# Two-expert routing: dense products over all tokens replaced by rows scattered to, and gathered from, per-expert parts of DRAM

## The chip, the core and the metric

One core of a Trainium2 chip runs the program. The metric is the device time of one execution in microseconds (us); the kernel before takes 2873.46 us, the median of 3 runs (2871.51 to 2873.73).

## The reference

A delta-rule attention (4 batches, 8 heads, 768 steps, head width 48) gives 3072 tokens of 384 numbers. A router chooses two of eight experts for each token, and each chosen expert adds its weighted two-layer product. All is float32.

```python
# attention, per step t
y[:, :, t] = einsum('bhd,bhde->bhe', q[:, :, t], state)
state = state + bt * einsum('bhd,bhe->bhde', kt, vt - v_old)
# router, N = 3072, D = 384, E = 8, F = 1024
noisy = x @ w_gate + log1p(exp(x @ w_noise)) * noise
top2 = argpartition(-noisy, 2, axis=1)[:, :2]        # softmax over the two: top2_w
for e in range(E):
    for k in range(2):
        mask = top2[:, k] == e
        h = maximum(x[mask] @ w1[e], 0.0)
        out[mask] += top2_w[mask, k, None] * (h @ w2[e])
```

The inputs are seeded. Counted from the reference on them, the eight experts are chosen by 711, 771, 789, 774, 756, 744, 807 and 792 tokens.

## The kernel before

Stage 1 is `deltanet` (lines 152 to 426): 24 groups (6 chunks of 128 tokens by 4 batches, the chunk the outer loop), three in flight at a time, advanced in turns by generators. For a group, `load` (186) brings k, q and v by SP's DMA queue into one of five buffer sets, `prepare` (202) normalizes the keys on POOL and VectorE (DVE), and `group` (240) builds an inverse of a 128 by 128 triangular matrix per head by merging blocks: TensorE (PE) products `p_m` (line 297) alternate with DVE operations that mask or add them (315, 305, 327). POOL adds the identity once a group (284). The group's result `y` is copied by ScalarE (ACT, 388), transposed on PE (`p_xt`, 394) and stored in `xT`, which holds all 3072 tokens, transposed, on chip.

Stage 2 is the router (lines 431 to 499): 72 products `p_l` (437), each of which PE runs as two instructions, then one chain of some 30 DVE and ACT operations on 128 by 24 by 8 numbers, which ends in `gate`, the weight of each expert for each token, 0 for all but two.

Stage 3 is the experts (lines 501 to 541): for each of 8 experts and each of 6 blocks of 512 tokens, the first product `p_h` (515; 24 products of 512 columns, 48 instructions) with a relu on ACT (521), then the second product `p_o` (526; 32 products of 384 columns, 64 instructions), which DVE adds to `acc` with the gate (532, 536). Weights of the next expert are loaded while one is computed (`load_weights`, 128). With the last expert each 128 tokens of `acc` are stored (541).

Each engine and each DMA-issuing queue runs its instructions in the order in which the scheduler of the framework wrote them; an instruction that waits holds those behind it. PSUM tiles (`ps`) rotate through 8 banks.

Of the kernel before, what the change touches and what calls it, by code (L numbers as in the profile page):

```python
# [20 lines left out]
TT = 512  # tokens in a tile of the experts' first product  # L21
# [3 lines left out]
def kernel(  # L25
# [49 lines left out]
    # 1 where the row is before the column  # L75
# [7 lines left out]
    # the two diagonal blocks of a pair of heads' state  # L83
# [5 lines left out]
    # -1 for rows in the lower block of a pair, by the columns of its upper block; 0 for  # L89
    # those of its lower block  # L90
# [16 lines left out]
    # -1 for even rows, by the next column  # L107
# [9 lines left out]
    # expert index less E, for the choice of the first of equal logits  # L117
# [4 lines left out]
    xT = const.tile([128, KT, N], FP32, name="xT")  # L122

# [28 lines left out]
    def deltanet(ictx):  # L152
# [31 lines left out]
        state = {}  # L184

# [22 lines left out]
            # normalized keys; a Newton step takes the square root to full precision  # L208
# [31 lines left out]
        def group(n):  # L240
# [4 lines left out]
            # two heads to a transpose  # L245
# [11 lines left out]
            # A^T, by parity of the heads: they stand in different rows of the array  # L257
# [13 lines left out]
            # the inverse of I + A, block by block, and its transpose  # L271
# [39 lines left out]
            for s in LEVELS:  # L311
                x = sb([128, H, 128], "x", IN_FLIGHT)  # - E T
# [19 lines left out]
            # strictly lower part of Q K^T, transposed  # L332
# [54 lines left out]
            y = sb([128, H, D], "y", 2)  # L387
# [7 lines left out]
            tok0 = b * S + c * C  # L395
            nc.scalar.copy(xT[:, :, tok0 : tok0 + C], p_xt)

        for n in range(n_sets):
            load(n)
        load_router()  # L400
        prepare(0)
# [30 lines left out]
    work = ctx.enter_context(tc.tile_pool(name="route", bufs=1))  # L432
    wgn, noise = router["wgn"], router["noise"]
    p_l = ps([128, NT, 2, E], "p_l")
    for t in range(NT):
        for do in range(KT):
            nc.tensor.matmul(  # L437
                p_l[:, t], xT[:, do, t * 128 : (t + 1) * 128], wgn[:, do],
                start=(do == 0), stop=(do == KT - 1),
            )  # L440

    def full(name):
        return work.tile([128, NT, E], FP32, name=name)

    def per_token(name):
        return work.tile([128, NT], FP32, name=name)

    def over_experts(t):
        return t[:, :, None].to_broadcast([128, NT, E])

    def vv(out, a, b, op):
        nc.vector.tensor_tensor(out=out, in0=a, in1=b, op=op)

    # log(1 + exp(z)) = max(z, 0) + log1p(exp(-|z|)); log1p corrected for 1 + u's rounding
    z_pos, u, w, d, noisy = (full(x) for x in ("z_pos", "u", "w", "d", "noisy"))
    nc.scalar.activation(u, p_l[:, :, 1], ACTF.Abs)
    nc.scalar.activation(u, u, ACTF.Exp, scale=-1.0)
    nc.vector.tensor_scalar_max(z_pos, p_l[:, :, 1], 0.0)
    nc.vector.tensor_scalar_add(w, u, 1.0)
    nc.vector.tensor_scalar_sub(d, w, 1.0)  # L460
    vv(d, u, d, ALU.subtract)
    nc.vector.reciprocal(noisy, w)
    vv(d, d, noisy, ALU.mult)
    nc.scalar.activation(w, w, ACTF.Ln)
    vv(w, w, d, ALU.add)
    vv(w, w, z_pos, ALU.add)
    vv(w, w, noise, ALU.mult)
    vv(noisy, w, p_l[:, :, 0], ALU.add)

    def take_largest(x, name):  # L470
        """The largest logit of each token, and 1 for the first expert that has it."""
        top, at, hit = per_token(f"{name}_top"), per_token(f"{name}_at"), full(f"{name}_hit")
        nc.vector.tensor_reduce(out=top, in_=x, axis=AX.X, op=ALU.max)
        vv(hit, x, over_experts(top), ALU.is_equal)
        code_b = code[:, None, :].to_broadcast([128, NT, E])
        vv(hit, hit, code_b, ALU.mult)
        nc.vector.tensor_reduce(out=at, in_=hit, axis=AX.X, op=ALU.min)
        vv(hit, code_b, over_experts(at), ALU.is_equal)
        return top, hit

    top0, hit0 = take_largest(noisy, "a")
    rest = full("rest")
    nc.vector.scalar_tensor_tensor(
        out=rest, in0=hit0, scalar=-1e30, in1=noisy, op0=ALU.mult, op1=ALU.add
    )
    top1, hit1 = take_largest(rest, "b")
    p1, den = per_token("p1"), per_token("den")
    vv(p1, top1, top0, ALU.subtract)
    nc.scalar.activation(p1, p1, ACTF.Exp)
# [4 lines left out]
    vv(p1, p1, den, ALU.mult)
    gate = full("gate")
    vv(gate, hit0, over_experts(den), ALU.mult)
    vv(hit1, hit1, over_experts(p1), ALU.mult)
    vv(gate, gate, hit1, ALU.add)

# [1 line left out]
    w_odd = ctx.enter_context(tc.tile_pool(name="w_odd", bufs=1))  # L501
    hid = ctx.enter_context(tc.tile_pool(name="hid", bufs=2))
    acc_pool = ctx.enter_context(tc.tile_pool(name="acc", bufs=1))
    acc = acc_pool.tile([128, NT, DM], FP32, name="acc")

    for e in range(E):
# [3 lines left out]
        for tt in range(N // TT):  # L510
            hT = hid.tile([128, FT, TT], FP32, name="hT")
            for fo in range(FT):
                p_h = ps([128, TT], "p_h")
                for do in range(KT):
                    nc.tensor.matmul(  # L515
                        p_h,
                        w1e[:, do, fo * 128 : (fo + 1) * 128],
                        xT[:, do, tt * TT : (tt + 1) * TT],
                        start=(do == 0), stop=(do == KT - 1),
                    )  # L520
                nc.scalar.activation(hT[:, fo], p_h, ACTF.Relu)  # L521
            for i in range(TT // 128):
                t = tt * (TT // 128) + i
                p_o = ps([128, DM], "p_o")
                for fo in range(FT):
                    nc.tensor.matmul(  # L526
                        p_o, hT[:, fo, i * 128 : (i + 1) * 128], w2e[:, fo],
                        start=(fo == 0), stop=(fo == FT - 1),
                    )
                g = gate[:, t, e : e + 1]  # L530
                if e == 0:
                    nc.vector.tensor_scalar(  # L532
                        out=acc[:, t], in0=p_o, scalar1=g, scalar2=None, op0=ALU.mult
                    )
# [38 lines left out]
```

## Time and profile before

| | us |
|---|---|
| median of 3 runs (2871.51 to 2873.73) | 2873.46 |
| span of the profiled execution, first to last instruction | 2872.1 |
| stage 1, delta rule, until the first product of the router | 855.9 |
| stage 2, router products on PE | 30.5 |
| stage 3, experts, until the last product | 1982.1 |
| PE busy | 2826.4 (98%) |
| DVE, ACT, POOL busy | 712.0, 340.0, 157.0 |

The profile is one execution on the chip. The span of the profiled execution is its own time but for 1.4 us, the difference to the median. A busy share is an average over stages with different limits, so a stage is read by the stretch of time that it takes. In the chain that ended last, a row is a piece of work of one engine which the next piece waited for.

### The profile page before, as it was taken

What the parts mean: (1) busy time and instruction counts of PE and PEld (TensorE: products, weight loads), DVE (VectorE), ACT (ScalarE), POOL (GpSimd) and SP (SyncE); (2) the same over time, 40 slices, a digit from 0 to 9 for tenths busy, and PEclk for the clock granted to TensorE, in tenths of its full rate; (3) what the DMA queues carried; (4) which work ended last, traced back from release to release, by engine and by line L of the source; (5) the groups of instructions that cost most, each with busy time, mean ns of one, the idle gap of its engine ahead of it and who ended that gap; (6) DMA issues with size and microseconds to landing.
All of it is one profiled execution on the core that took longest, in us unless ns stands there. A gap on an engine that the chain in (4) does not pass through costs nothing.

```text
span 2872.1 us, 28617 instructions
## 1 busy us (share of the span) xinstructions
PE 2826.4 (98%) x12894; PEld 1849.6 (64%) x12894; DVE 712.0 (25%) x1279; ACT 340.0 (12%) x610; POOL 157.0 (5%) x183
## 2 busy tenths in 40 slices
PE   5999999999999999999999999999999999999999
PEld 5999999999996555555555555555555555555555
DVE  5766677777651000000000000000000000000000
ACT  1111111111101110011001101110111011101110
POOL 3111221111000000000000000000000000000000
PEclk9999999999997999999999999999999999999999
DMA  5010100000000001000100100000010000000000
GB/s 94 18 23 18 21 18 18 18 18 12 1 22 23 0 1 44 0 0 0 44 0 0 44 0 0 22 22 1 0 44 0 0 22 22 0 0 6 17 22 22
DMA packets 93915, 46.10 MB, mean 16 GB/s; under 512 B 79424, under 2 KB 90688, under 8 KB 93792
## 3 DMA queue, kind: packets, MB, share of 16 engines
q1 hardware_dynamic: 93792, 44.27, 5.9%
q8 instruction: 101, 1.65, 0.2%
q14 instruction: 22, 0.18, 0.0%
HBM read 39.54 MB, written 4.72 MB: 15 GB/s over the span
## 4 chain that ended last, share of the span: by engine, by line
PE 93%; DVE 3%; POOL 2%; issue 1%; ACT 0%; POOLq 0%; DVEq 0%; ACTq 0%
PE p_h L515 35%; PE p_o L526 34%; PE p_m L297 17%; POOL w_inv L284 2%; PE p_g L265 2%; PE p_u L354 1%; PE p_l L437 1%; DVE w_inv L278 1%; PE p_t L250 1%; DVE t_inv L290 1%; PE p_b L347 1%; ACT at L277 0%; PE p_xt L394 0%; PE p_y L382 0%; DVE w_inv L327 0%
## 5 line engine op out<-in xcount | busy, mean ns | idle before, releaser
L515 PE MATMUL p_h<-xT,w1e 128*128 128x512 f32 x2304 | 999.1, 593 | 0.0
L526 PE MATMUL p_o<-w2e,hT 128*128 128x384 f32 x3072 | 998.6, 486 | 0.0
L526 PEld LDWEIGHTS p_o<-w2e,hT 128*128 128x128 f32 x3072 | 583.8, 190 | 417.1 <-issue 23.0
L515 PEld LDWEIGHTS p_h<-xT,w1e 128*128 128x128 f32 x2304 | 438.7, 190 | 541.9 <-issue 529.5
L536 DVE SCALAR_TENSOR_TENSOR acc<-p_o,gate,acc 128x384 f32<-128x384 f32 x168 | 103.8, 618 | 1628.3 <-PE p_o L526 1628.3
L521 ACT ACTIVATE hT<-p_h 128x512 f32<-128x512 f32 x384 | 229.3, 597 | 1727.3 <-PE p_h L515 1727.3
L297 PE MATMUL p_m<-t_inv,at 128*128 128x128 f32 x2304 | 283.4, 279 | 25.3 <-DVE t_inv L290 25.3
L297 PEld LDWEIGHTS p_m<-t_inv,at 128*128 128x128 f32 x2304 | 269.9, 194 | 29.2 <-issue 29.2
L297 PE MATMUL p_m<-x,w_inv 128*128 128x128 f32 x1920 | 233.3, 277 | 1.4 <-DVE x L315 1.4
L297 PEld LDWEIGHTS p_m<-x,w_inv 128*128 128x128 f32 x1920 | 222.4, 192 | 2.6 <-DVE x L315 2.0
L315 DVE TENSOR_TENSOR x<-p_m,neg 128x512 f32<-128x512 f32 x288 | 195.9, 686 | 107.6 <-PE p_m L297 107.4
L327 DVE STREAM_TRANSPOSE w_inv<-t_inv 128x1024 f32<-128x1024 f32 x96 | 119.2, 1242 | 2.1
L305 DVE TENSOR_TENSOR t_inv<-p_m,t_inv 128x256 f32<-128x256 f32 x240 | 96.4, 414 | 52.2 <-PE p_m L297 50.4
L297 PE MATMUL p_m<-w_inv,x 128*128 128x128 f32 x768 | 93.7, 275 | 0.0
L297 PEld LDWEIGHTS p_m<-w_inv,x 128*128 128x128 f32 x768 | 89.6, 192 | 0.1
L532 DVE TENSOR_SCALAR acc<-p_o,gate 128x384 f32<-128x384 f32 x24 | 14.8, 618 | 221.4 <-PE p_o L526 221.4
L252 ACT COPY kT<-p_t 128x512 f32<-128x512 f32 x24 | 14.2, 591 | 468.3 <-PE p_t L250 468.3
L284 POOL TENSOR_TENSOR w_inv<-w_inv,ident 128x1024 f32<-128x1024 f32 x24 | 56.4, 2352 | 155.5 <-DVE w_inv L278 153.7
L382 PE MATMUL p_y<-u,qk 128*128 128x48 f32 x384 | 47.5, 278 | 0.0
L382 PEld LDWEIGHTS p_y<-u,qk 128*128 128x128 f32 x384 | 46.5, 198 | 0.0
L305 DVE TENSOR_TENSOR w_inv<-p_m,w_inv 128x256 f32<-128x256 f32 x96 | 37.7, 411 | 18.7 <-PE p_m L297 18.7
L354 PE MATMUL p_u<-r,w_inv 128*128 128x48 f32 x320 | 37.8, 271 | 0.8 <-DVE r L349 0.8
(109 smaller groups left out, 820.2 us busy)
## 6 DMA issues: line engine op xcount, KB each, us to landing
w1e<-in_moe_w_dram SPq DMA_DIRECT2D x8, 1536.0 KB, 6.4
w2e<-in_moe_w_dram SPq DMA_DIRECT2D x8, 1536.0 KB, 7.1
kp<-in_k_dram SPq DMA_DIRECT2D x24, 192.0 KB, 2.8
qp<-in_q_dram SPq DMA_DIRECT2D x24, 192.0 KB, 2.8
vr<-in_v_dram SPq DMA_DIRECT2D x24, 192.0 KB, 2.7
out_dram<-acc SPq DMA_DIRECT2D x24, 192.0 KB, 1.9
beta_sb<-in_beta_dram SPq DMA_DIRECT2D x1, 96.0 KB, 2.2
noise<-in_moe_noise_dram SPq DMA_DIRECT2D x1, 96.0 KB, 3.8
```

The costliest lines, as they stand in the source:

```text
L265: nc.tensor.matmul(p_g[par][:, j], kT[lo : lo + DP, j], rhs[lo : lo + DP, j])
L284: nc.gpsimd.tensor_tensor(out=w_inv, in0=w_inv, in1=ident[:, None, :].to_broadcast([128, H, 128]), op=ALU.add,)
L297: nc.tensor.matmul(p[:, i], lhsT[:, h0 + i], rhs[:, h0 + i])
L305: nc.vector.tensor_tensor(out=to, in0=halves(p, s)[low], in1=to, op=ALU.add)
L315: lambda p, hs: nc.vector.tensor_tensor(out=x[:, hs], in0=p, in1=neg[s][:, None, :].to_broadcast([128, NP, 128]), op=ALU.mult,),
L327: nc.vector.transpose(out=w_flat, in_=t_flat)
L354: nc.tensor.matmul(p_u[:, h], w_inv[:, h], r[:, h])
L382: nc.tensor.matmul(p_y[:, h], qk[:, h], u[:, h], start=(st is None and h == 0), stop=(h == H - 1), skip_group_check=True,)
L515: nc.tensor.matmul(p_h, w1e[:, do, fo * 128 : (fo + 1) * 128], xT[:, do, tt * TT : (tt + 1) * TT], start=(do == 0), stop=(do == KT - 1),)
L521: nc.scalar.activation(hT[:, fo], p_h, ACTF.Relu)
L526: nc.tensor.matmul(p_o, hT[:, fo, i * 128 : (i + 1) * 128], w2e[:, fo], start=(fo == 0), stop=(fo == FT - 1),)
L536: nc.vector.scalar_tensor_tensor(out=acc[:, t], in0=p_o, scalar=g, in1=acc[:, t], op0=ALU.mult, op1=ALU.add,)
```

## The change

`TILES` is 7, `HALF` 448 and `TT` 512. The router moves into stage 1, where it runs once per chunk (512 tokens), and the experts multiply only the rows sent to them.

- `rows_x` and `rows_y` are DRAM buffers of 8 parts with 3072 rows of 384 numbers. `clear` (new) writes zeros to the first 896 rows of each part of `rows_x` and to the other 2176 rows of each part of `rows_y`: 64 stores, 24576 rows of 1536 bytes, issued by SP after the router's loads and ahead of the first weights.
- `group` ends with its own 3 router products `p_l`. With the last batch of a chunk, `route` (new) runs the router's chain on 128 by 4 by 8 numbers, finds each token's row among its expert's rows (`before` counts the earlier ones; two products `p_at` with a triangular and an all-ones matrix count those of the same chunk), and `spread` (new) sends `y` by 8 indirect DMAs of 128 rows each, issued by POOL. `xT` is 3 buffers of one group instead of all tokens; `y` has 8 buffers.
- An expert loads its 896 rows (`xr`), which waits for all 48 scatters, transposes them by 21 PE transposes, and runs the first product on two halves of 448 columns (48 products) and the second on 7 tiles (56 products of 384 columns). DVE copies each result, and SP stores it to `rows_y`.
- A branch for experts with over 896 rows: every engine loads the largest count and, if it is above 896, the other 17 tiles of each of the 8 experts are computed.
- At the end POOL gathers, for each of 24 tiles of tokens, two tiles of 128 rows by indirect DMAs; ACT and DVE weight and add them, and SP stores them.

```diff
+    def clear(e):
+        for i in range(TILES):
+            r0 = e * N + i * 128
+            cleared.append(nc.sync.dma_start(out=rows_x[r0 : r0 + 128], in_=zero).ins)
+        left = rows_y[e * N + TILES * 128 : (e + 1) * N]
+        nc.sync.dma_start(out=left.rearrange("(t p) d -> p t d", p=128),
+            in_=zero[:, None, :].to_broadcast([128, NT - TILES, DM]))
+    def spread(rows, slot):
+        d = nc.gpsimd.indirect_dma_start(out=rows_x,
+            out_offset=bass.IndirectOffsetOnAxis(ap=slot, axis=0),
+            in_=rows, in_offset=None).ins
...
+        for i in cleared:
+            tc.add_manual_dep(d, i.name, SYNC, reason="rows cleared before they are written")
+        def route(c):
...
+            vv(taken, hit0, hit1, ALU.add)
+            for i in range(B):
+                nc.vector.tensor_copy(earlier[:, i], before)
+                vv(before, before, taken[:, i], ALU.add)
+            nc.tensor.matmul(p_at, mask_u, taken, start=True, stop=False)
+            nc.tensor.matmul(p_at, ones, earlier, start=False, stop=True)
+            vv(at, p_at, part[:, None, :].to_broadcast([128, B, E]), ALU.add)
+            for hit, slot in ((hit0, slots[0]), (hit1, slots[1])):
+                vv(mine, hit, at, ALU.mult)
+                nc.vector.tensor_reduce(out=row, in_=mine, axis=AX.X, op=ALU.add)
+                nc.vector.tensor_copy(slot[:, to], row)
+            for b in range(B):
+                for slot in slots:
+                    spread(ys[n], slot[:, n : n + 1])
...
-            nc.scalar.copy(xT[:, :, tok0 : tok0 + C], p_xt)
+            nc.scalar.copy(xT, p_xt)
+            for do in range(KT):
+                nc.tensor.matmul(p_l, xT[:, do], wgn[:, do], ...)
+            nc.scalar.copy(logits[c][:, b], p_l)
+            if b == B - 1:
+                route(c)
...
         load_router()
+        for e in range(E):
+            clear(e)
         prepare(0)
         first_weights = load_weights(w_even, 0)
...
     for e in range(E):
-        for tt in range(N // TT):
...
+        d = nc.sync.dma_start(out=xr, in_=rows_x[rows].rearrange("(t p) d -> p t d", p=128)).ins
+        for i in written:
+            tc.add_manual_dep(d, i.name, SYNC, reason="rows of all tokens")
+        for i in range(TILES):
+            transposed(xr, xe, i)
+        for h0 in range(0, TILES * 128, HALF):
+            first(w1e, xe, hT, slice(h0, h0 + HALF))
+        for i in range(TILES):
+            second(w2e, hT, i, yr)
+            nc.sync.dma_start(out=rows_y[r0 : r0 + 128], in_=yr)
+    count = nc.values_load(most_i[0:1, 0:1], min_val=0, max_val=N)
+    with tc.If(count > TILES * 128):
...
+    for c in range(NCH):
+        for b in range(B):
+            for slot in slots:
+                nc.gpsimd.indirect_dma_start(out=g, in_=rows_y, ...)
+            nc.scalar.mul(got[0], got[0], gates[0][:, n : n + 1])
+            nc.vector.scalar_tensor_tensor(out=got[0], in0=got[1], scalar=gates[1][:, n : n + 1], ...)
+            nc.sync.dma_start(out=out[t0 : t0 + C, :], in_=got[0])
```

How the order moves, at three places. First, SP's queue at the start, before (`w1e` and `w2e` are the weights of expert 0; `qp`, `vr` and `kp` behind them belong to group 5 and later):

```order
L146 DMA noise<-in_moe_noise_dram 128x24x8
L131 DMA w1e<-in_moe_w_dram 128x3x1024
L132 DMA w2e<-in_moe_w_dram 128x8x384
L191 DMA qp_124<-in_q_dram 128x8x48
L191 DMA qp_128<-in_q_dram 128x8x48
L191 DMA qp_132<-in_q_dram 128x8x48
L191 DMA vr<-in_v_dram 128x8x48
L191 DMA kp_123<-in_k_dram 128x8x48
```

The same place in the change, from the last of the eight pairs of clearing rows on:

```order
L186 DMA rows_x<-zero 128x384 x7
L188 DMA rows_y<-zero 128x17x384
L159 DMA w1e<-in_moe_w_dram 128x3x1024
L160 DMA w2e<-in_moe_w_dram 128x8x384
L334 DMA kp_145<-in_k_dram 128x8x48
L334 DMA qp_146<-in_q_dram 128x8x48
L334 DMA vr<-in_v_dram 128x8x48
```

All 64 clearing stores stand ahead of the weights and of the loads of group 5; each DMA of SP also waits for the landing of the one that stands eight before it.

Second, PE where the last group of the first chunk ends, before (`p_m` belongs to the next two groups):

```order
L394 MATMUL p_xt<-ident,y 128x128 x3
L297 MATMUL p_m<-t_inv,at 128x128 x8
L297 MATMUL p_m<-x,w_inv 128x128 x16
L297 MATMUL p_m<-w_inv,x 128x128 x8
L297 MATMUL p_m<-t_inv,at 128x128 x16
```

and in the change:

```order
L537 MATMUL p_xt<-ident,y 128x128 x3
L440 MATMUL p_m<-t_inv,at 128x128 x8
L440 MATMUL p_m<-x,w_inv 128x128 x8
L545 MATMUL p_l<-wgn,xT 128x16 x3
L306 MATMUL p_at<-r_taken,mask_u 128x32
L440 MATMUL p_m<-x,w_inv 128x128 x2
L307 MATMUL p_at<-r_earlier,ones 128x32
L440 MATMUL p_m<-x,w_inv 128x128 x6
L440 MATMUL p_m<-w_inv,x 128x128 x8
L440 MATMUL p_m<-t_inv,at 128x128 x16
```

The product `p_at` stands right behind `p_l`, so PE waits there for `r_taken`, which 24 DVE operations of the chain compute behind `p_l`; on DVE the chain's 41 operations stand together, with one transpose of another group among them, and the `t_inv` additions that the last row's products need come behind them. The same happens in five chunks; in the sixth nothing else is left to do.

Third, SP where the experts begin, in the change:

```order
L334 DMA kp_157<-in_k_dram 128x8x48
L159 DMA w1e<-in_moe_w_dram 128x3x1024
L160 DMA w2e<-in_moe_w_dram 128x8x384
L625 DMA xr<-rows_x 128x7x384 x3
L159 DMA w1e<-in_moe_w_dram 128x3x1024
L640 DMA rows_y<-yr 128x384 x6
```

The weights of expert 1 take memory that stage 1 held, and their load waits for all its readers, the scatters too; the rows of experts 0, 1 and 2 stand behind these weights, two experts ahead of their use from then on.

## Rows read from the trace of the kernel before

**Rows 1.** The page: span, and busy time of each engine.

```profile
span 2872.1 us, 28617 instructions
...
PE 2826.4 (98%) x12894; PEld 1849.6 (64%) x12894; DVE 712.0 (25%) x1279; ACT 340.0 (12%) x610; POOL 157.0 (5%) x183
```

**Rows 2.** Chain that ended last, by time: start us, us, work.

```profile
855.90 30.53 PE p_l L437 x144
886.43 23.09 PE p_h L515 x48
909.52 20.64 PE p_o L526 x64
930.16 20.60 PE p_h L515 x48
...
2847.80 20.66 PE p_o L526 x64
```

**Rows 3.** Windows: busy us (count) of PE, PEld, DVE, ACT, POOL; clock; DMA; GB/s.

```profile
200.00:300.00 100.00, 99.28 (x913) 97.34 (x912) 71.02 (x129) 12.85 (x27) 18.80 (x17) 1.00 0.10 19
...
850.00:870.00 20.00, 19.37 (x94) 19.21 (x93) 0.00 (x0) 1.22 (x3) 0.00 (x0) 0.50 0.45 157
```

**Rows 4.** Groups by line and form: busy us, mean ns, idle before.

```profile
L297 PE MATMUL p_m<-t_inv,at 128*128 128x128 f32 x2304 | 283.4, 279 | 25.3 <-DVE t_inv L290 25.3
...
L437 PE MATMUL p_l<-wgn,xT 128*128 128x16 f32 x144 | 30.7, 373 | 0.0
...
L394 PE MATMUL p_xt<-ident,y 128*128 128x128 f32 x72 | 12.2, 280 | 0.6 <-ACT y L388 0.6
...
L388 ACT COPY y<-p_y 128x384 f32<-128x384 f32 x24 | 11.5, 479 | 61.8 <-PE p_y L382 61.8
```

**Rows 5.** Timeline of the router's chain on DVE and ACT: start us, us, instruction.

```profile
886.60 0.33 ACT L456 ACTIVATE u<-p_l 128x192 f32<-128x192 f32 x1 [30.18 <-PE p_l L437]
886.95 1.28 ACT L457 ACT_TABLE_LOAD   x1
...
892.15 1.28 ACT L464 ACT_TABLE_LOAD   x1
...
900.39 0.36 DVE L452 TENSOR_TENSOR gate<-gate,b_hit 128x192 f32<-128x192 f32 x1
```

**Rows 6.** Timeline of DVE in stage 1: two dependent small operations.

```profile
94.30 0.16 DVE L220 TENSOR_TENSOR rec<-rec,ss 128x8 f32<-128x8 f32 x1
94.50 0.17 DVE L221 TENSOR_TENSOR rec<-rec,root 128x8 f32<-128x8 f32 x1
```

**Rows 7.** Timeline of POOL in stage 1.

```profile
88.39 0.82 POOL L210 TENSOR_TENSOR ksq<-kp 128x384 f32<-128x384 f32 x1 [0.30 <-DMA kp<-in_k_dram]
...
178.71 0.83 POOL L231 TENSOR_TENSOR kb<-kp,beta_t 128x384 f32<-128x384 f32 x1 [15.72 <-PE p_t L250]
...
219.85 2.35 POOL L284 TENSOR_TENSOR w_inv<-w_inv,ident 128x1024 f32<-128x1024 f32 x1 [5.36 <-DVE w_inv L278]
...
232.21 0.83 POOL L227 TENSOR_TENSOR kp<-kp,ksc 128x384 f32<-128x384 f32 x1 [8.26 <-DVE ksc L226]
247.04 0.83 POOL L231 TENSOR_TENSOR kb<-kp,beta_t 128x384 f32<-128x384 f32 x1 [14.01 <-PE p_t L250]
```

**Rows 8.** SP's DMA issues at the start: start us, us, what is loaded.

```profile
19.38 2.00 SPq L131 DMA_DIRECT2D w1e<-in_moe_w_dram  x1
...
84.86 0.37 SPq L191 DMA_DIRECT2D kp<-in_k_dram  x1
```

**Rows 9.** DMA of the window 855 to 875 us: rate in 40 slices, issues, us to landing.

```profile
GB/s 0 0 0 0 131 66 238 401 418 410 418 442 410 373 402 396 375 381 369 369 384 298 12 0 0 0 0 0 0 0 0 0 0 0 0 33 0 0 0 0
...
w2e<-in_moe_w_dram SPq DMA_DIRECT2D x1, 1536.0 KB, 10.2
```

**Rows 10.** Line 541, the output's stores: issue ns min/median/max, and time to landing.

```profile
L541 SPq DMA_DIRECT2D out_dram<-acc x24: 332/332/366, 2647.4 to 2869.1; - x24
...
DMA to landing us min/median/max: 1.8/1.9/2.0
```

**Rows 11.** The page's DMA issues: KB each, median us from issue to landing.

```profile
kp<-in_k_dram SPq DMA_DIRECT2D x24, 192.0 KB, 2.8
```

More of the change, by code (lines that the diff above doesn't have):

```diff
@@ L149, in load_router @@
         router["wgn"], router["noise"] = wgn, noise
+    cleared, written = [], []
+    def clear(e):
[3 more added lines that the diff above has]
+        left = rows_y[e * N + TILES * 128 : (e + 1) * N]
+        nc.sync.dma_start(
+            out=left.rearrange("(t p) d -> p t d", p=128),
+            in_=zero[:, None, :].to_broadcast([128, NT - TILES, DM]),
+        )
+    def spread(rows, slot):
+        d = nc.gpsimd.indirect_dma_start(
+            out=rows_x,
+            out_offset=bass.IndirectOffsetOnAxis(ap=slot, axis=0),
+            in_=rows,
+            in_offset=None,
+        ).ins
+        tc.declare_no_dep(d, group="spread", reason="no two tokens have the same row")
+        tc.add_to_no_dep_group("spread", d)
+        for i in cleared:
+            tc.add_manual_dep(d, i.name, SYNC, reason="rows cleared before they are written")
+        written.append(d)
     def deltanet(ictx):
@@ L400, in deltanet @@
         load_router()
+        for e in range(E):
+            clear(e)
         prepare(0)
@@ L429, with transposed @@
         weights = deltanet(ictx)
[L432 to L435, printed above, removed]
+    w_odd = ctx.enter_context(tc.tile_pool(name="w_odd", bufs=1))
+    moe = ctx.enter_context(tc.tile_pool(name="moe", bufs=2))
+    def transposed(xr, xe, i):
+        p_xt = ps([128, KT, 128], "p_xt")
         for do in range(KT):
+            nc.tensor.transpose(p_xt[:, do], xr[:, i, do * 128 : (do + 1) * 128], ident)
+        nc.vector.tensor_copy(xe[:, :, i * 128 : (i + 1) * 128], p_xt)
@@ new lines, in first, with second @@
+    def first(w1e, xe, hT, cols):
+        for fo in range(FT):
+            p_h = ps([128, cols.stop - cols.start], "p_h")
+            for do in range(KT):
+                nc.tensor.matmul(
+                    p_h, w1e[:, do, fo * 128 : (fo + 1) * 128], xe[:, do, cols],
+                    start=(do == 0), stop=(do == KT - 1),
+                )
+            nc.scalar.activation(hT[:, fo, cols], p_h, ACTF.Relu)
+    def second(w2e, hT, i, yr):
+        p_o = ps([128, DM], "p_o")
+        for fo in range(FT):
@@ L455 @@
[L455 to L465, printed above, removed]
@@ L494 @@
[L494 to L504, printed above, removed]
+                p_o, hT[:, fo, i * 128 : (i + 1) * 128], w2e[:, fo],
@@ L506 @@
+                start=(fo == 0), stop=(fo == FT - 1),
+            )
+        nc.vector.tensor_copy(yr, p_o)
     for e in range(E):
@@ L509 @@
             weights = load_weights(w_odd if e % 2 == 0 else w_even, e + 1)
-        for tt in range(N // TT):
[L511 to L534, printed above, removed]
-                else:
-                    nc.vector.scalar_tensor_tensor(
-                        out=acc[:, t], in0=p_o, scalar=g, in1=acc[:, t],
-                        op0=ALU.mult, op1=ALU.add,
-                    )
-                if e == E - 1:
-                    nc.sync.dma_start(out=out[t * 128 : (t + 1) * 128, :], in_=acc[:, t])
@@ new lines @@
+    nc.vector.tensor_reduce(out=most, in_=p_n, axis=AX.X, op=ALU.max)
+    nc.vector.tensor_copy(most_i, most)
+    count = nc.values_load(most_i[0:1, 0:1], min_val=0, max_val=N)
+    with tc.If(count > TILES * 128):
+        more = NT - TILES
+        w1f = moe_w1.rearrange("e d f -> (e d) f")
+        w2f = moe_w2.rearrange("e f d -> (e f) d")
+        for e in range(E):
+            with tc.tile_pool(name=f"left{e}", bufs=1) as pool:
+                w1e = pool.tile([128, KT, F], FP32, name="w1l")
+                w2e = pool.tile([128, FT, DM], FP32, name="w2l")
+                nc.sync.dma_start(out=w1e, in_=w1r[e])
+                nc.sync.dma_start(out=w2e, in_=w2r[e])
+                for i in range(TILES, NT):
+                    r0 = e * N + i * 128
+                    xr = pool.tile([128, 1, DM], FP32, name="xrl")
+                    nc.sync.dma_start(out=xr[:, 0], in_=rows_x[r0 : r0 + 128])
+                    xe = pool.tile([128, KT, 128], FP32, name="xel")
+                    transposed(xr, xe, 0)
+                    hT = pool.tile([128, FT, 128], FP32, name="hTl")
+                    first(w1e, xe, hT, slice(0, 128))
+                    yr = pool.tile([128, DM], FP32, name="yrl")
+                    second(w2e, hT, 0, yr)
+                    nc.sync.dma_start(out=rows_y[r0 : r0 + 128], in_=yr)
```

151 lines of the change are left out of this document (112 added, 39 removed).

## Prediction

> **What bounds the kernel now.** I read the page first: PE is busy for 98% of the span [rows 1]. A share over the whole span says little, so the chain by time comes next [rows 2]. From 855.90 us on there is one piece of PE work behind another: the router's products until 886.43, then blocks of 20.60 us (`p_h`) and 20.64 us (`p_o`) that alternate, 48 of each, until 2868.46. That is 1982 us of experts, or 69% of the span, with nothing but PE in the chain. Last come the windows by stage [rows 3]: in stage 1 PE is busy for 99.28 of 100 us while DVE has 71.02 and POOL 18.80, so PE sets the pace there too, but only because the other engines come back in time. Small transfers, POOL and ACT cost nothing now. The change takes most of the PE work away and puts waits between engines in its place, so the question is how much of 1982 us the waits give back.
>
> **What goes.** Everything after 855.90 us [rows 2], 2016.2 us of the profiled span.
>
> **The experts that come.** Work is now 896 rows an expert and not 3072. A block's 24 products of 512 columns take 20.60 us; 48 products of 448 columns take 2 x 20.60 x 448/512 = 36.05 us. 32 products of 384 columns take 20.64 us; 56 take 36.12 us. 21 transposes at 12.2 us / 72 = 0.17 us [rows 4] are 3.6 us. With 0.6 us until the first copies of the transposed rows are there, an expert is 76.4 us and eight are 611 us. Loads and copies beside it are covered: rows and weights come two experts ahead, and 5.9 MB in 76 us is 78 GB/s where 369 to 442 GB/s are to be had [rows 9]. If that cover went, an expert would wait up to 10.2 us, a weight load's landing. After a stretch at clock 0.50 [rows 3], the lower of the two levels (1.2 GHz), the first block took 23.09 us in place of 20.60 [rows 2]; PE idles before the experts again, so I add 2.5 us. **614 us.**
>
> **The router's products inside stage 1.** 144 instructions in 30.7 us at clock 0.50 [rows 3, 4] are 0.21 us each, so some 0.107 at full clock, 15.3 us in all on PE, which has no room. With 12 small `p_at`: **16 us.** Bounds: 8 us if gaps take half of it, 31 at the low clock.
>
> **The chain that PE waits for in five chunks.** PE stands at `p_at` right behind `p_l`. Before it come ACT's copy and Abs (0.3 us each) and a table load of 1.28 us [rows 5], Exp (0.3), 24 DVE operations and a wait of some 0.7 us for the second table. Dependent DVE operations of 8 columns follow each other at 0.20 us (94.30 to 94.50 [rows 6]); for 32 columns I take 0.22, so 5.3 us. That is 8.2 us. The other 16 operations (3.5 us) still hold DVE while PE has 16 products, 3.9 us at 2 x 0.123 (283.4/2304 [rows 4]), so they hide. Behind DVE's chain are the other groups' additions; I add 2 us for catching up: 10 us, **50 us** for five. Bounds: 5 us a chunk if other work fills half; 14.2 us, the whole chain of before (886.60 to 900.75 [rows 5]).
>
> **The scatters on POOL.** The trace has no indirect DMA. The nearest rows are 0.33 us, SP's issue of as many bytes in as many rows [rows 10], and 2.8 us, a load of that size from issue to landing [rows 11]. POOL has to make 128 row addresses a time; its own instructions take 0.83 us for 128 by 384 and 2.35 for the largest [rows 7], and I take 1.4 us, between these two. Eight are 11.2 us and stand between `kp` (ends 233.0) and `kb` (247.0) [rows 7], a gap of 14 us, so within stage 1 they cost **0**. Behind them on POOL wait `kb`, `vr` and `w_inv`, and behind `w_inv` DVE and then PE; at 2.8 us eight are 22.4 and up to 8 us a chunk would show.
>
> **The clearing stores at the start.** 24576 rows of 1536 bytes are 37.75 MB. They start at 19.4 us [rows 8] in the weights' old place. The weight load at 856 us, partly rows of 1536 bytes too, runs at about 390 GB/s [rows 9]: 97 us, done at 116; weights 8 us, group 5's loads landed at 128. Stores one by one at 1.9 us [rows 10] would be 103 GB/s, 365 us, done at 385. I take the fast end, as eight may be under way. Group 5's load is issued at 84.86 now [rows 8] and its square starts at 88.39; but PE reads the group only just before 178.71, when POOL gets the buffer back [rows 7]. With 6 us of preparing, loads may land until 171: 43 us of slack, so **0**. The stall begins below 37.75 MB / 140 us = 270 GB/s.
>
> **The end of stage 1, now in the open.** Before, the router's chain lay beside `p_h`. Now nothing can: the last `p_l` 0.6, the whole chain 12.2 us, 8 scatters 11.2, landing 2.5, then SP's queue, where the weights of expert 1 (3.15 MB) stand ahead of `xr` (1.38 MB): 4.5 MB at 390 GB/s and 2 us, 13.6. **40 us**; 28 to 55 by the bounds of the scatter.
>
> **The tail.** After the last product a copy 0.6, a store 1.9 [rows 10] and the branch: every engine loads a number and jumps over a long body. No row shows a branch; 0 to 10 us, I take 5. Then 48 gathers on POOL at 1.4 = 67.2 us. The bytes alone (9.4 MB at 390 GB/s) are 24 us, so 24 is the low end and 48 x 2.8 = 134 the high one. The last tile: 2.8 landing, ACT's 0.48 for 128 by 384 [rows 4], DVE's 0.6, the store 1.9. **81 us.**
>
> The Trainium skill, page "DMA: Bandwidth & Descriptors", section "Anatomy of one DMA — SWDGE (gpsimd) path", fits 2.0 us plus bytes/436e3 per DMA that POOL issues, 2.45 us for 196,608 bytes, an estimate by that page which no run here shows; by it, if gathers follow one by one, the tail's 67 us would be 118.
>
> **Sum.** 855.9 + 16 + 50 + 0 + 0 + 40 + 614 + 81 = 1656.9 us of span; the median lies 1.4 us above the span of before, so **1658 us**.
>
> **The rivals.**
> - *POOL's indirect DMAs set the end.* If each holds POOL until its rows have landed, 2.8 us [rows 11], the tail grows by 48 x 1.4 = 67 us, the last scatters by 11, and five chunks by 8 each: 1658 + 118 = 1776. For it: 48 gathers stand alone on one queue. Against it: eight buffers let them overlap. The skill's fit above lies near. Chance 0.20.
> - *The clearing holds back group 5.* At 200 GB/s the loads land at 19 + 189 + 11 = 219, 48 us late: 1706. At 103 GB/s they land at 395, 224 late: 1882. For it: no row shows a long write to DRAM. Against it: half the rate of [rows 9] is needed before anything shows. Chance 0.14, most of it near 1706.
> - *The issue is cheap and the chain hides.* Scatter and gather at 0.33 us: 24 us of gathers, 43 less, the last scatters 9 less, chunks at 5 us, 25 less: 1581. For it: SP issues as much in 0.33 us. Chance 0.12.
> - *Slower than before: the branch is taken.* Then 17 more tiles of all 8 experts run: 136 tiles of 24 x 2 x 0.123 + 5.16 + 0.5 = 11.6 us, 1572 us, and 8 weight loads that nothing covers, 85 us: 1658 + 1657 = 3315, 441 us slower. It decides at one expert with more than 896 tokens; the choices counted from the reference go to 807, so only a wrong count could take it. Chance 0.01.
>
> **How the numbers follow.** Forecast 0.53, rivals as above. The likeliest case alone spans 1600 to 1720. The range of 1590 to 1785 takes in the POOL rival and the milder clearing, and leaves out the cheap-issue end, the slow clearing and the branch, with what lies beyond in both directions. All cases but the branch are faster by far more than 0.2%, about what a measurement of this kernel can tell from no change: faster 0.99, same 0.00, slower 0.01.
>
> **What would show it.** In the changed profile: an expert period near 76 us with PE busy throughout; five gaps of PE of some 10 us in stage 1, released by DVE at `p_at`; no wait for group 5's loads near 178 us; one idle stretch of PE of some 40 us before the experts; at the end some 70 us in which POOL issues gathers 1.4 us apart and PE is silent. I am wrong if the experts' period is set by a DMA, if the first 250 us show PE waiting for `kp` or `vr`, or if the tail is over 150 us.

## The result and the profile after

The kernel after the change takes 1640.42 us (median of 4 runs, 1639.66 to 1641.27), the one before 2873.6 (2871.51 to 2874.08): a ratio of 0.571 [0.570, 0.572]. The profiled execution of the new kernel has a span of 1637.8 us. The forecast was 1658 us; the time lies inside the range, and the forecast's own case is the one that came.

The page of the new kernel, against [rows 1]: PE's share fell from 98% to 88%.

```profile
span 1637.8 us, 21932 instructions
...
PE 1445.1 (88%) x9376; PEld 1163.7 (71%) x9376; DVE 701.6 (43%) x1454; ACT 226.3 (14%) x440; POOL 250.3 (15%) x279
```

PE's timeline at the end of stage 1 and through the first experts (start us, us, instruction, in brackets the idle time before it and what ended it) answers to [rows 2]:

```profile
921.68 0.84 PE L545 MATMUL p_l<-wgn,xT 128*128 128x16 f32 x6 [0.62 <-ACT xT L539]
...
959.87 4.53 PE L597 MATMUL p_xt<-ident,xr 128*128 128x128 f32 x21 [29.59 <-DMA xr<-rows_x]
964.24 36.25 PE L604 MATMUL p_h<-xe,w1e 128*128 128x448 f32 x96
1000.32 36.28 PE L613 MATMUL p_o<-w2e,hT 128*128 128x384 f32 x112
1036.44 2.46 PE L597 MATMUL p_xt<-ident,xr 128*128 128x128 f32 x21
1039.11 36.35 PE L604 MATMUL p_h<-xe,w1e 128*128 128x448 f32 x96 [0.21 <-DVE xe L598]
1075.30 36.28 PE L613 MATMUL p_o<-w2e,hT 128*128 128x384 f32 x112
1111.42 2.46 PE L597 MATMUL p_xt<-ident,xr 128*128 128x128 f32 x21
```

The last `p_l` starts at 921.68 us, where before the router began at 855.90. From there to the first transposes of an expert it is 38.2 us, in which PE has only the two `p_at`. Between the second and the third expert lie 1111.42 - 1036.44 = 74.98 us, in which PE waits only 0.21 us, for DVE's copy `xe`. The first takes 1.6 us more, most of it in the transposes (4.53 us for 2.46).

The tail, in the timelines of DVE and POOL:

```profile
1561.46 0.56 DVE L617 COPY yr<-p_o 128x384 f32<-128x384 f32 x1 [4.60 <-PE p_o L613]
```

```profile
1567.92 0.98 POOL L679 DMA_INDIRECT got<-rows_y,slot  x1 [626.10 <-PEq L650]
1569.21 0.97 POOL L679 DMA_INDIRECT got<-rows_y,slot  x1 [0.30 <-issue]
...
1628.12 0.95 POOL L679 DMA_INDIRECT got<-rows_y,slot  x1 [0.47 <-issue]
```

The forecast's terms can be read off at these points:

| stretch | forecast | after |
|---|---|---|
| up to the last `p_l` | 855.9 + 16 + 50 = 921.9 | 921.7 |
| last `p_l` to the first transpose of an expert | 40 | 38.2 |
| experts, until the last copy of a result (1561.46) | 614 | 601.6 |
| tail, from that copy on | 81 | 76.3 |
| span | 1656.9 | 1637.8 |

### The profile page after: what moved, and what is told of

Its sections match the earlier page's. It is cut to its first block, busy times and chain, and to the rows that moved or that the text cites. A ratio compares the mean times of both kernels' runs of the same rounds, so it can differ in the third digit from the quotient of the medians.

```text
span 1637.8 us, 21932 instructions
## 1 busy us (share of the span) xinstructions
PE 1445.1 (88%) x9376; PEld 1163.7 (71%) x9376; DVE 701.6 (43%) x1454; ACT 226.3 (14%) x440; POOL 250.3 (15%) x279
## 5 line engine op out<-in xcount | busy, mean ns | idle before, releaser
L604 PE MATMUL p_h<-xe,w1e 128*128 128x448 f32 x768 | 290.7, 540 | 1.5 <-DVE xe L598 1.5
L613 PE MATMUL p_o<-w2e,hT 128*128 128x384 f32 x896 | 290.3, 486 | 0.0
L617 DVE COPY yr<-p_o 128x384 f32<-128x384 f32 x56 | 31.2, 558 | 543.0 <-PE p_o L613 543.0
L613 PEld LDWEIGHTS p_o<-w2e,hT 128*128 128x128 f32 x896 | 170.2, 190 | 119.6 <-issue 3.0
L604 PEld LDWEIGHTS p_h<-xe,w1e 128*128 128x128 f32 x768 | 145.3, 190 | 142.9 <-issue 139.7
L679 POOL DMA_INDIRECT got<-rows_y,slot x48 | 46.4, 967 | 640.8 <-PEq L650 626.1
L608 ACT ACTIVATE hT<-p_h 128x448 f32<-128x448 f32 x128 | 69.7, 544 | 528.4 <-PE p_h L604 528.4
L194 POOL DMA_INDIRECT rows_x<-y,slot x48 | 46.9, 977 | 127.7 <-issue 117.1
L374 POOL TENSOR_TENSOR kb<-kp,beta_t 128x384 f32<-128x384 f32 x24 | 19.9, 829 | 242.3 <-PE p_t L393 242.1
L597 PE MATMUL p_xt<-ident,xr 128*128 128x128 f32 x168 | 21.7, 290 | 29.6 <-DMA xr<-rows_x 29.6
```

The lines of the kernel that those rows point to most:

```text
L194: d = nc.gpsimd.indirect_dma_start(out=rows_x, out_offset=bass.IndirectOffsetOnAxis(ap=slot, axis=0), in_=rows, in_offset=None,).ins
L597: nc.tensor.transpose(p_xt[:, do], xr[:, i, do * 128 : (do + 1) * 128], ident)
L604: nc.tensor.matmul(p_h, w1e[:, do, fo * 128 : (fo + 1) * 128], xe[:, do, cols], start=(do == 0), stop=(do == KT - 1),)
L608: nc.scalar.activation(hT[:, fo, cols], p_h, ACTF.Relu)
L613: nc.tensor.matmul(p_o, hT[:, fo, i * 128 : (i + 1) * 128], w2e[:, fo], start=(fo == 0), stop=(fo == FT - 1),)
L617: nc.vector.tensor_copy(yr, p_o)
```

## The experiments

Times are compared with the 1640.4 us of the changed kernel. All edits are against it.

**Where the router's product stands (e1_spread).** `route` becomes a generator, which the turn loop advances.

```diff
-                route(c)
+                routes.append(route(c))
...
             active = still
+            routes[:] = [g for g in routes if next(g, DONE) is not DONE]
```

> The router of a chunk is made a generator that the turn loop advances beside the groups, in six pieces, so that the product p_at stands some 30 rows behind p_l on PE and the chain's DVE operations lie between those of other groups; nothing is left out. Theory A (the place of p_at in PE's queue is what costs 10.3 us in each of five chunks): PE has other work while the chain runs, p_at waits for less than 1 us, and 40 to 50 us of 51 come back: 1590 to 1602 us, 1595 likeliest. Rival B (the 41 DVE operations, about 8 us a chunk, and ACT's two table loads are work that the groups in flight must wait for wherever it stands): PE's waits go from p_at to p_m, and less than 20 us come back: 1621 to 1640 us.

Measured: 1607.7 us (1603.3 to 1608.7), 32.7 less, between the two. In the kernel of the change, PE's rows at the first chunk's end and the windows (busy us and count of PE, PEld, DVE, ACT, POOL; granted clock; DMA share; GB/s) show what was to be removed:

```profile
197.94 0.74 PE L545 MATMUL p_l<-wgn,xT 128*128 128x16 f32 x6
205.97 0.61 PE L306 MATMUL p_at<-r_taken,mask_u 128*128 128x32 f32 x2 [7.29 <-DVE gate L255]
```

```profile
200.00:202.00 2.00, 0.00 (x0) 0.00 (x0) 1.11 (x6) 1.96 (x3) 0.00 (x0) 1.00 0.00 0
202.00:204.00 2.00, 0.00 (x0) 0.00 (x0) 1.50 (x8) 1.51 (x2) 0.00 (x0) 0.73 0.00 0
204.00:208.00 4.00, 2.03 (x9) 2.06 (x10) 3.14 (x22) 0.20 (x1) 0.00 (x0) 0.50 0.01 2
208.00:210.00 2.00, 2.00 (x12) 2.00 (x12) 1.23 (x8) 0.00 (x0) 0.40 (x1) 0.57 0.00 0
210.00:212.00 2.00, 2.00 (x21) 2.00 (x20) 0.85 (x2) 0.00 (x0) 1.70 (x2) 1.00 0.29 100
```

PE stands still for 7.29 us, and what follows runs at a clock of 0.50. A good measure of a chunk's cost is the interval between the starts of two of POOL's additions of the identity (`w_inv`), one a group. It was 34.17 us before, and is 34.83 after within a chunk and 44.53, 45.08, 45.36, 45.51 and 45.58 across the five chunk ends, so 10.4 us more on average. The first of these five in the changed kernel, and the first long interval in this run, one group later:

```profile
188.39 2.36 POOL L427 TENSOR_TENSOR w_inv<-w_inv,ident 128x1024 f32<-128x1024 f32 x1 [1.23 <-DVE w_inv L421]
232.92 2.35 POOL L427 TENSOR_TENSOR w_inv<-w_inv,ident 128x1024 f32<-128x1024 f32 x1 [4.21 <-DVE w_inv L421]
```

```profile
223.41 2.35 POOL L433 TENSOR_TENSOR w_inv<-w_inv,ident 128x1024 f32<-128x1024 f32 x1 [3.31 <-DVE w_inv L427]
261.67 2.36 POOL L433 TENSOR_TENSOR w_inv<-w_inv,ident 128x1024 f32<-128x1024 f32 x1 [5.36 <-DVE w_inv L427]
```

In this run it is 38.26, 38.23, 37.98 and 37.97 for the first four chunks and 35.14 for the fifth. So 7 us came back in each of the four, and 3.4 did not. Those have a cause that neither theory named. POOL and DVE in this run, behind the first chunk:

```profile
236.78 0.97 POOL L195 DMA_INDIRECT rows_x<-y,slot  x1 [0.30 <-issue]
237.77 0.84 POOL L359 TENSOR_TENSOR ksq<-kp 128x384 f32<-128x384 f32 x1
```

```profile
238.65 0.55 DVE L363 TENSOR_REDUCE ss<-ksq 128x8 f32<-128x384 f32 x1 [5.62 <-POOL ksq L359]
239.12 0.75 DVE L454 TENSOR_TENSOR t_inv<-p_m,t_inv 128x256 f32<-128x256 f32 x2
```

The square `ksq` of the next group's keys stands behind the eight scatters in POOL's queue; DVE, in order too, waits 5.62 us for it, and behind that wait stand the `t_inv` additions that PE's next products need. In the changed kernel the scatters stand between `kp` and `kb`, and POOL then still waits 6.26 us for PE before `kb`. The edit moved them with the end of the chain, so it is their new place, ahead of `ksq`, that costs. In the fifth chunk no `ksq` of a later group stands behind them, and there the interval is only 0.3 us longer than within a chunk, though fewer groups are in flight there too. The row of the changed kernel:

```profile
225.95 0.82 POOL L374 TENSOR_TENSOR kb<-kp,beta_t 128x384 f32<-128x384 f32 x1 [6.26 <-PE p_t L393]
```

The place does not cost the whole 3.4 us. PE's waits behind the first chunk are 1.26 us for these additions, 0.53 for an `x` 4 us later, when DVE catches up, and, ahead of both, 0.81 for DVE's transpose `t_inv`. This last one comes from the chain: while POOL added the identity (223.41 to 225.76), one of the chain's small operations, `r_mine`, held DVE for 2.10 us, where it takes 0.19 in the changed kernel:

```profile
223.71 2.10 DVE L256 TENSOR_TENSOR r_mine<-r_a_hit,r_at 128x32 f32<-128x32 f32 x1
```

These waits are 2.6 of the 3.4 us; the two `p_at` add some 0.5 of work on PE.

At the last addition of the identity this run is 38.0 us ahead of the changed kernel. Of these, 3.4 go again before the sixth chunk's `p_at`: the granted clock is 0.50 from 880 to 890 us, where the changed kernel has 1.00 in its last group.

**The clock (e5_warm).**

```diff
+            for i in range(28):
+                nc.tensor.matmul(p_w[:, i % 4], ident, mask_u)
             p_at = ps([128, B, E], "p_at")
```

> Ahead of each p_at PE gets 28 extra products of 128 by 128 (identity by mask, read by nobody), about 28 x 2 x 0.123 = 6.9 us at full clock, which fit into the wait of 7.3 us there; nothing else changes. Theory A (of 10.3 us a chunk some 3 are PE's and the groups' work at the granted clock of 0.50 to 0.73 that follows the idle wait): the clock stays at 1.00 through the wait, and 5 x 2 to 3 us come back: 1625 to 1631 us. Rival B (the part beyond the wait is the other groups' DVE additions, which stand behind the chain): 1638 to 1645 us.

Measured: 1630.5 us (1628.2 to 1631.0), 9.9 less: theory A. The windows of this run, at the same place, have the clock at 1.00 throughout:

```profile
200.00:204.00 4.00, 4.00 (x38) 4.00 (x37) 2.57 (x15) 3.28 (x5) 0.00 (x0) 1.00 0.01 4
204.00:208.00 4.00, 3.06 (x27) 2.90 (x26) 3.59 (x25) 0.20 (x1) 0.00 (x0) 1.00 0.01 2
```

At the first chunk end `p_at` now waits 0.94 us behind the idle products. The interval across a chunk end is 42.75 to 42.79 us in all five. So of 10.4 us a chunk, 2.4 are work at the low clock and 8.0 the wait for the chain. At the last addition of the identity this run is 12.4 us ahead. Of these, 2.0 go again in the last group, where its clock is 0.56 from 905 to 911 us (1.00 in the changed kernel's last group), and 0.9 between the last `p_l` and the transposes. Work that nobody reads made the kernel faster.

**Whose work the rest is (e11_best_pool).** On top of e10_best (below), two-operand operations of the chain go to POOL in the first five chunks (17 by the trace).

```diff
-                nc.vector.tensor_tensor(out=out, in0=a, in1=b, op=op)
+                eng = nc.gpsimd if c < NCH - 1 and op != ALU.is_equal else nc.vector
...
+                eng.tensor_tensor(out=out, in0=a, in1=b, op=op)
```

> As the run before, and in the first five chunks those two-operand operations of the router's chain that add, subtract or multiply two tiles (19 of 41 a chunk) run on POOL in place of DVE. Theory A (the 3.4 us a chunk that the spread router still costs are the groups' DVE operations waiting behind the chain's): half or more of 17 us comes back, 1579 to 1588 us. Rival B (POOL's queue, with the chain in it, hands out kb and w_inv later, and what DVE gives back is lost): 1594 to 1606 us.

Measured: 1592.7 us (1592.2 to 1594.5), 4.3 less than e10_best and short of both theories. The first two long intervals are 37.52 and 37.33, 0.8 and 0.9 less than in e10_best. That is the wait of 0.81 us for `t_inv`, which is gone here: `r_mine` runs on POOL, ahead of the identity. The row on DVE is the same as above, with a wait of 5.86 us for `ksq`, which again stands right behind the scatters, and PE's waits of 1.50 and 0.53 us remain. That fits the reading of e1: most of what is left is the scatters' place on POOL, not the chain's work on DVE. No run moved the scatters back, so this is read from the traces and not shown by an edit.

**Twice the clearing (e2_double_clear).** `clear(e)` is called twice for each expert.

> All 64 clearing stores are issued twice, 75.5 MB in place of 37.7, with nothing else changed. Theory A (the clearing is hidden only because group 5's loads, issued at 121 us and landed some 16 us later, still come before about 171 us): at the 95 us that one clearing took SP, the loads are issued at about 217 and land near 233 us, some 60 us too late: 1700 us, 1685 to 1715. Rival B (the stores run beside the loads on other DMA engines, or the slack is larger than worked out): 1640 to 1650 us.

Measured: 1715.7 us (1715.5 to 1715.9), 75.3 more: theory A, a little above its range. The keys of group 5 on SP's queue and on POOL, PE's longest wait (us in total, times, longest), and two windows:

```profile
224.74 5.83 SPq L334 DMA_DIRECT2D kp<-in_k_dram  x1
```

```profile
240.92 0.82 POOL L353 TENSOR_TENSOR ksq<-kp 128x384 f32<-128x384 f32 x1 [83.63 <-DMA kp<-in_k_dram]
```

```profile
PE p_t L393 <- POOL kp L370: 64.0, 1, 64.0
```

```profile
60.00:100.00 40.00, 38.87 (x355) 38.22 (x355) 27.02 (x44) 4.25 (x9) 3.18 (x2) 0.99 1.03 365
210.00:230.00 20.00, 0.00 (x0) 0.00 (x0) 0.00 (x0) 0.00 (x0) 0.00 (x0) 0.50 1.03 353
```

The DMA engines are full (1.03) at 353 to 365 GB/s, PE works on untouched until its input is missing, and then waits 64 us. POOL could begin at 240.9, so without a wait of PE it might have begun as late as 240.9 - 64.0 = 176.9, an estimate; the forecast had put the last landing that costs nothing at 171. In the changed kernel one clearing leaves PE alone:

```profile
19.00:115.00 96.00, 79.18 (x684) 77.24 (x682) 63.72 (x103) 10.31 (x22) 13.86 (x12) 0.98 1.03 357
```

PE is busy for 79.18 us in this window in the kernel before too:

```profile
19.00:115.00 96.00, 79.18 (x689) 77.25 (x688) 64.52 (x110) 10.83 (x23) 17.18 (x16) 0.98 0.19 48
```

**Clearing later (e9_late_yclear).** The stores of `left` move from `clear` into the expert loop of the source.

> The eight large clearing stores of rows_y (26.7 of 37.7 MB) are issued from the expert loop's place in the program, so that in SP's queue they stand behind the loads of group 5 and of later groups; nothing is left out. Theory A (the clearing at the start costs only the 2.7 us by which group 5 came late): 1637.7 us, 1636 to 1639. Rival B (it costs more, because its writes slow the other transfers of the first 130 us): 1625 to 1635 us. Rival C (moved, the stores only come in the way of later loads): 1640 to 1650 us.

Measured: 1653.9 us (1650.7 to 1658.0), 13.5 more: more than any theory had, and for another reason. In the trace SP issues the eight stores from 57.6 us on, the last at 155, so they are later but still in stage 1, and the clearing is over well before the first chunk end.

First, theory A's 2.7 us were mostly misread. The sixth addition of the identity comes at 185.68 us in the kernel before, at 188.39 in the changed one and at 187.68 in this run. So 2.0 of the 2.7 us stay without the early clearing: three groups that had each grown by some 0.66 us of router products. The clearing had 0.7 in it.

Second, the loss lies at the chunk ends: 47.05, 48.98, 47.00, 47.07 and 46.92 us, 11.0 more over the five than in the changed kernel. The order of the work does not explain it: from 190 us on, through all five chunk ends, PE, DVE, ACT and POOL carry out the same operations in the same order in both kernels. About 1 us at the first chunk end is the clock, which stays at 0.56 in 210 to 212 us where it was 1.00 above. The rest shows as DVE taking up finished products late while the scatters run (DVE busy for 1.36 of 4 us, 3.06 in the changed kernel); the cause stayed open (see e12).

```profile
210.00:212.00 2.00, 2.00 (x13) 2.00 (x12) 0.72 (x2) 0.00 (x0) 1.39 (x3) 0.56 0.37 134
216.00:220.00 4.00, 3.34 (x30) 3.15 (x29) 1.36 (x2) 0.00 (x0) 2.38 (x3) 1.00 0.43 160
```

**Rows before weights (e4_xr_first).** In the expert loop `load_weights` for the next expert moves behind the load of `xr`.

> In the expert loop the rows xr are loaded ahead of the next expert's weights in SP's queue, so the rows of expert 0 no longer stand behind 3.1 MB; nothing is left out. Theory A (the stretch of 38 us ahead of the experts has 10 us in which xr only waits for the weights to pass): xr lands some 6 us behind the last scatter in place of 16, and the stretch is 28 to 30 us: 1631 us, 1629 to 1633. Rival B (the two loads share the DMA engines whatever their order, or the landing of the last scatter sets the time): 1638 to 1641 us.

Measured: 1631.7 us (1631.2 to 1632.5), 8.7 less: theory A.

```profile
923.13 0.84 PE L545 MATMUL p_l<-wgn,xT 128*128 128x16 f32 x6 [0.62 <-ACT xT L539]
...
952.08 4.06 PE L597 MATMUL p_xt<-ident,xr 128*128 128x128 f32 x21 [20.34 <-DMA xr<-rows_x]
```

From the last `p_l` to the transposes it is 28.95 us now, and the load of `xr`, issued at 945.45, is there 6.6 us later.

**One more tile (e3_tiles8).** `TILES = 8`.

> TILES is 8 and HALF 512: each expert multiplies 1024 rows in place of 896; the bytes cleared stay the same and nothing is left out. Theory A (an expert is as long as its PE work, 75.0 us for 7 tiles, so 10.7 us a tile): 8 x 10.7 = 86 us more, 1726 us, and a period of 85.7 us. Rival B (part of the period is fixed: copies, loads, waits between the engines): 40 to 65 us more, 1680 to 1705 us.

Measured: 1724.3 us (1723.0 to 1725.7), 83.9 more: theory A. PE's rows of the third expert:

```profile
1133.05 2.78 PE L597 MATMUL p_xt<-ident,xr 128*128 128x128 f32 x24
1135.72 41.47 PE L604 MATMUL p_h<-xe,w1e 128*128 128x512 f32 x96
1177.03 41.44 PE L613 MATMUL p_o<-w2e,hT 128*128 128x384 f32 x128
1218.31 2.78 PE L597 MATMUL p_xt<-ident,xr 128*128 128x128 f32 x24
```

The period is 85.26 us for 8 tiles and 74.98 for 7: 10.66 and 10.71 a tile. From the first transpose to the first product it is 2.67 us with either number, and the products are 10.3 us a tile. So an expert is as long as its PE work.

**What a gather costs (e6_gather64).** Half of the tokens get other rows in this run, as its expectation says.

```diff
-                nc.gpsimd.indirect_dma_start(out=g, ..., slot[:, n : n + 1]
+                for p0 in (0, 64):
+                    nc.gpsimd.indirect_dma_start(out=g[p0 : p0 + 64], ..., slot[0:64, n : n + 1]
```

> Each tile of the final gather is brought by two indirect DMAs of 64 rows, 96 in place of 48 with as many rows and bytes; the second DMA of each pair fetches the first one's rows again, so half of the tokens get other rows. Theory A (a gather costs POOL by its rows, 0.97 us for 128, and 0.30 us between two): 96 x (0.48 + 0.30) = 75 us in place of 61, so 1654 us, 1650 to 1660. Theory B (a fixed cost for each indirect DMA, whatever its rows): 96 x 1.26 = 121 us, 1700 us, 1690 to 1705. Theory C (bytes or landing set the pace): 1638 to 1643 us.

Measured: 1692.8 us (1691.5 to 1694.5), 52.4 more: theory B. The gathers by form (ns min/median/max, first and last start) in the changed kernel and in this one:

```profile
L679 POOL DMA_INDIRECT got<-rows_y,slot x48: 947/954/1185, 1567.9 to 1628.1; - x48
...
DMA to landing us min/median/max: 3.0/3.8/5.1
```

```profile
L680 POOL DMA_INDIRECT got<-rows_y,slot x96: 901/907/922, 1569.6 to 1684.8; - x96
```

64 rows hold POOL for 0.907 us and 128 for 0.954: half the rows save 0.05 us. The starts lie 1.21 us apart here and 1.28 there. No other size was run.

**Twice the scatters (e12_double_scatter).** Each `spread` is followed by the same indirect DMA into `rows_d`.

> Each scatter is followed by a second one of the same rows into another DRAM buffer that nobody reads, 96 in place of 48. In the open stretch before the experts 7 more stand ahead of the last one that counts, 7 x 1.27 = 8.9 us. In each of the five chunks before, POOL is free some 4.2 us later than it now begins kb. Theory A (the scatters of these chunks lie in a gap of POOL that nobody waits for): 1649 us, 1648 to 1654. Rival B (PE waits for kb as soon as it is late): 5 x 4.2 us more, 1665 to 1673 us.

Measured: 1718.1 us (1715.1 to 1722.1), 77.7 more, far beyond both theories. The open stretch behaved as said: PE's wait for `xr` grew from 29.6 to 39.4 us. But the intervals across chunk ends are 57.69, 60.39 and 57.53 us in the first three, 12 to 15 more each. The wait is not for `kb`: POOL is through with the scatters at 230.3 us and then itself waits 9.24 us for PE before it can begin `kb`. The scatters hold POOL from 210.0 us on, at 1.27 us each, and in that time PE and DVE falter, in the windows of this run and, below, of the changed kernel:

```profile
220.00:225.00 5.00, 2.79 (x19) 2.30 (x19) 2.08 (x3) 0.00 (x0) 3.78 (x5) 1.00 0.42 155
225.00:230.00 5.00, 2.04 (x8) 1.28 (x9) 0.42 (x1) 0.00 (x0) 3.78 (x5) 0.77 0.41 152
```

```profile
216.00:220.00 4.00, 4.00 (x38) 4.00 (x37) 3.06 (x6) 0.00 (x0) 2.91 (x3) 1.00 0.40 148
```

The changed kernel's window has scatters too, and nothing slows. In the doubled run the trace names no engine that PE and DVE wait for:

```profile
227.76 0.42 DVE L457 TENSOR_TENSOR w_inv<-p_m,w_inv 128x256 f32<-128x256 f32 x1 [3.22 <-remote]
```

```profile
224.40 1.01 PE L417 MATMUL p_g<-qT,kT 64*128 64x128 f32 x4
227.02 0.40 PE L417 MATMUL p_g<-qT,kT 64*128 64x128 f32 x3 [1.61 <-issue]
```

What slows the two engines there could not be settled: it begins 10 us after the first scatter, and e9 shows a mild form of it. Longer loads of instructions do not show: their queue moved two packets between 205 and 240 us in this run and in the changed kernel.

**The branch (e7_no_branch, e8_branch_taken).** In e7 everything from `most` to the end of the `If` is left out.

> The count, its load into every engine and the branch over the other 17 tiles are left out; nothing of it runs on these inputs. Theory A (of 6.0 us between the last copy of a result and the first gather, the last store's landing is 1.9 and the branch the rest): 4 us less, 1636 us, 1635 to 1638. Rival B (the branch is decided beside the last products and the wait is the store and POOL's queue): less than 1.5 us, 1639 to 1641 us.

Measured: 1638.5 us (1637.5 to 1639.6), 2.0 less, between the theories. That is little to go by, as the median of the kernel before moves by 2.2 us between the sets of runs (2871.67 to 2873.87). The trace says more: in this run the last copy starts at 1562.48 and the first gather at 1566.09 us, 3.6 us apart; with the branch it is 6.5. So the count, its load and the branch cost 2 to 3 us, and the rest is the last store's landing and POOL's start.

In e8:

```diff
-    with tc.If(count > TILES * 128):
+    with tc.If(count > 768):
```

> The branch's bound is 768 rows in place of 896, so that it is taken on these inputs; the clearing covers all rows of rows_x and none of rows_y, as many bytes as before. Theory A (a tile of 128 rows is as long as its PE work, 11.6 us, and a weight load of 10.6 us stands open for each expert): 136 x 11.6 + 85 = 1657 us more, 3297 us, 3230 to 3380. Rival B (with one buffer of each kind, a tile's load, copies and relus stand open too, 2 to 4 us a tile): 3500 to 3850 us. Either way slower than the kernel of before by 350 us or more.

Measured: 3389.0 us (one run), 1748.6 more, and some 515 slower than the kernel of before. PE's rows in the branch:

```profile
1640.93 5.62 PE L605 MATMUL p_h<-xel,w1l 128*128 128x128 f32 x48 [0.79 <-DVE xel L599]
...
1651.55 0.49 PE L598 MATMUL p_xt<-ident,xrl 128*128 128x128 f32 x3
1652.83 5.62 PE L605 MATMUL p_h<-xel,w1l 128*128 128x128 f32 x48 [0.78 <-DVE xel L599]
```

A tile is 11.90 us (11.6 expected), so 136 are 1618. PE's waits for weights and rows come to 98 us in 7 pieces, 14 each where 10.6 was expected. Theory A's account fits, but its 3297 us were 92 too low, and the time lies just outside its range; 32 us of what the branch adds were not taken apart.

**Together (e10_best).** The edits of e1, e4 and e9 in one kernel.

> Three edits together: the router of a chunk spread over the turns (32.7 us less by itself), xr ahead of the next weights (8.7 us less by itself) and the late clearing of rows_y (about 2.7). If they are independent, 1640.4 - 32.7 - 8.7 - 2.7 = 1596 us, 1594 to 1599. Rival (with the router out of the way, DMAs or POOL become the wait in stage 1): 1600 to 1608 us.

Measured: 1597.0 us (1595.8 to 1597.8), a ratio to the kernel of before of 0.556 [0.555, 0.557]. The gains of e1 and e4 add up: 1640.4 - 32.7 - 8.7 = 1599.0. The late clearing, harmful alone, is worth at most some 2 us here, where PE no longer stands at `p_at`. With e11's edit it is 1592.7, 0.554 [0.553, 0.555]: the fastest version run, and still 47.8 us below the changed kernel.

## Why the prediction was right, point by point

The parts that miss, the experts by 12.4 us, the tail by 4.7 and the end of stage 1 by 1.8, were all put too high. Only the chain's agreement is in part luck.

- *What goes, and the experts that come.* Right in kind: e3 shows that an expert is PE's work. Of the 12.4 us that the term was too high, 9 are the transposes, 2.46 us where 3.6 was put: the 12.2/72 of [rows 4] come from threes, and three in a row take 0.49 us (0.16 each) in the rows of e8, 21 take 2.46 (0.117 each). 3 more are the first copies, 0.21 for 0.6 us, and 0.9 the low clock at the start, 1.6 for 2.5. The products came to 72.3 us for 72.2 forecast, which takes back 1.
- *The router's products.* 0.66 us a group and 15.8 in all, for 16.
- *The chain in five chunks.* 10.4 us a chunk for 10. The parts were not right: 8.2 of waiting and 2 of other engines catching up were forecast; it is 8.0 of waiting and 2.4 of low clock (e5). The forecast counted the low clock ahead of the experts, but not behind these waits; that its 2 us fit is luck.
- *The scatters at nothing.* 1.27 us each for 1.4. They stand in the gap that the forecast named, and behind them POOL still waits 6.26 us for PE before `kb`. That holds for this place only (e1). The allowance of "8 us a chunk" at twice the time was too small: doubled, they cost 12 to 15 (e12), and not by way of `kb`.
- *The clearing at nothing.* 357 GB/s for 390, PE unchanged at 79.18 of 96 us, and a last landing that e2 puts at 176.9 for the forecast's 171. By e9 it costs 0.7 us and not 0. The rival's "half the rate" does not fit the forecast's own bound, 270 GB/s, which is 69% of 390; the measured rate is clear of both.
- *The end of stage 1.* 38.2 for 40: up to the first scatter 10.2 us for 12.8, the scatters 9.9 for 11.2, then 2.2 until SP issues the weights for 2.5, and from there until `xr` is there 15.9 for 13.6. e4 took 8.7 of it away.
- *The tail.* 76.3 for 81. Gathers start 1.28 us apart for 1.4; the branch costs 2 to 3 us for 5. From the start of the last gather to the last operation on ACT it is 4.3 us, where 1.4 + 2.8 were put, and from the issue of the last store to the end 4.0 for 1.9.
- *The rivals.* POOL does not wait for a gather's landing: a median of 3.8 us to landing stands beside starts 1.28 us apart. The fit of the Trainium skill, page "DMA: Bandwidth & Descriptors", section "Anatomy of one DMA — SWDGE (gpsimd) path", 2.45 us for such a DMA, is not the interval here; eight buffers overlap, and the landing itself is longer. The clearing did not hold back group 5; issue was not as cheap as 0.33 us; the branch, forced, gave 3389 us where 3315 was worked out.

## What to carry to other kernels

A wait placed right behind its producer in an in-order queue costs the whole chain between them, and on TensorE the slow clock after it; move the consumer down the queue first (32.7 us here; part of the chain on another engine then gave 4.3). An operation that is free in one place of a queue need not be in another, and an edit that moves a chain moves what hangs on its end: look what stands behind that in its new place. Indirect DMAs were paid by the piece on the engine that issues them (64 rows against 128), so make each as large as the form allows.

## What was not expected of the hardware

- PE's granted clock was 1.00 until 202 us and 0.50 from 204 on, after PE had stood still since 198.7; filling the wait with idle products kept it at 1.00 and took 9.9 us off the kernel.
- While POOL added the identity for 2.35 us, a small DVE operation took 2.10 us in place of 0.19, and ended with it (e1).
- An indirect DMA of 64 rows holds POOL nearly as long as one of 128: 0.907 and 0.954 us.
- With 16 scatters in a row, PE and DVE lost 12 to 15 us a chunk at waits for which the trace names no engine; with the 8 of the changed kernel nothing of the kind shows, with the 8 of e9 a mild form. The cause stays open.
